# One exponential moved ahead of K's high part in ACT's queue

## The chip, the cores and the metric

The kernel runs on one core of a Trainium2 chip. The metric is device time in microseconds (us). Five engines have queues of their own and work through them strictly in order: PE (TensorE, matmuls and transposes), DVE (VectorE), ACT (ScalarE), POOL (GpSimd) and SP (which here issues DMAs). What one engine makes and another uses is guarded by semaphores.

## The reference

Attention with RMS-normed queries and keys, followed by two gated MLPs on its output:

```
q_n, k_n = rmsnorm(q, g_q), rmsnorm(k, g_k)        # 4 x 12 heads, 448 x 64
scores = 1/8 * q_n @ k_n^T
attn = exp(scores - max(scores)) ; attn /= sum(attn) + 1e-9
x = attn @ v                                       # seen as 1792 x 768
x = ((x @ w_a) * (x @ w_b)) @ w_out                # 768 -> 1536 -> 768
x = (sigmoid(x @ w_gate) * (x @ w_val)) @ w_out    # the result
```

All is float32. A float32 product is made on PE from a high and a low part of each factor (three matmuls: high by high, high by low, low by high).

## The kernel before

The attention takes two heads at a time, as a pair; there are 24 pairs. Pair i's seven score tiles of 128 queries are called t = 0 to 6: PE makes tiles t and t + 4 together in `s(i, t)` (line 373), DVE takes each tile's row maximum in `top` (line 379), and ACT takes the exponential with its row sum in `exp` (line 392). A score tile lies in one of three PSUM buffers, so the third tile after it can be begun only when its exponential is done.

K and Q of the next pair are prepared meanwhile. `t_tr(i, 1)` transposes K and `t_tr(i, 0)` transposes Q on PE into a PSUM tile `tr`; for K, ACT then takes the high part, `k_hi` (line 341, tile `KH`), and DVE the low part, `k_lo` (line 352, tile `KL`), which reads KH. For Q the same is done at lines 331 (`q_hi`) and 336 (`q_lo`).

The exponentials of the pair before are turned and multiplied with V. `x_tr(i, j)` transposes a block of them on PE (14 transposes, into another `tr`), `x_out(i, j, b)` copies the result to SBUF in two halves, tile `pt` (ACT at line 426; for two of the six halves DVE at line 424), and `pv(i, j)` multiplies it with V (line 438). All `tr` tiles come from one pool of two PSUM buffers (`ps_tr`, `bufs=2`), so each transposing step waits until what lay in its buffer has been copied out or read.

The rest of a pair is small: `total`, `rsum` and `rsum_tr` make the inverse row sums, `norm` (line 477, tile `xs`) scales a result of two pairs before, `mean` (line 253), `rsqrt` and `newton` (lines 275 to 277) make the norms of a pair two or three ahead, POOL scales Q and K (lines 286 and 299) and squares them (lines 229 to 231). `decode` puts one step of preparing the MLPs' weights (lines 724 to 731, 844, 658) on ACT or DVE, where a planner chooses.

The order of all this is written out by hand. A turn is one pass of the table `turns`, which runs for i = 2 to 22, so 21 times; in it, offset 0 is the pair whose scores are made, 1 the pair whose K and Q are prepared, -1 the pair whose exponentials are turned. Each engine gets its instructions in the table's order. The tools place the semaphore waits, and pick which of a pool's buffers a tile gets.

```
(early, 0), (early_hi, -1), (squares, 3), (total, -1), (early_lo, -1), (s, 0, 0), (t_tr, 1, 1),
(top, 0, 0), (k_hi, 1), (exp, 0, 0), (x_tr, -1, 0), (top, 0, 4), (k_lo, 1), (x_out, -1, 0, 0), (s, 0, 1),
(x_out, -1, 0, 1), (norm, -2), (rsum, -1), (decode, 0, 0), (mean, 3), (exp, 0, 4), (x_tr, -1, 1), (x_out, -1, 1, 0),
```

These are the first three rows of the table. After them come x_out(-1, 1, 1) on DVE, top(0, 1) and exp(0, 1), and so on to tile 3.

Of the kernel before, what the change touches and what calls it, by code (L numbers as in the profile page):

```python
# [23 lines left out]
def attention_then_two_gated_mlps(  # L24
# [90 lines left out]
    def attention():  # L115
# [418 lines left out]
        def warm(i, n):  # L534
# [28 lines left out]

        turns = (
            (early, 0), (early_hi, -1), (squares, 3), (total, -1), (early_lo, -1), (s, 0, 0), (t_tr, 1, 1),
            (top, 0, 0), (k_hi, 1), (exp, 0, 0), (x_tr, -1, 0), (top, 0, 4), (k_lo, 1), (x_out, -1, 0, 0), (s, 0, 1),
            (x_out, -1, 0, 1), (norm, -2), (rsum, -1), (decode, 0, 0), (mean, 3), (exp, 0, 4), (x_tr, -1, 1), (x_out, -1, 1, 0),
            (load, 4), (load_r, 3), (load_v, 1), (t_tr, 1, 0), (rsum_tr, -1), (rsum_post, -1), (put, -2),
            (pv, -1, 0), (scale, 2, 2), (x_out, -1, 1, 1), (top, 0, 1), (q_hi, 1), (scale, 2, 0), (exp, 0, 1), (pv, -1, 1),
# [836 lines left out]
    with tc.manual_schedule():  # L1406
        main = mlps()
        attention()
        open_places(6, 4, 2, 3)
        begin_mm("mm1", 3)  # L1410
        for c in range(KC):
            place(where[0]["A22"], "l", c, F32, "f")
        for n, c in (("A22", 0), ("A21", 0), ("A22", 1), ("A21", 1), ("A21", 2), ("A22", 2)):
            stage_in(0, n, c)
        for c in range(KC):
            stage_in(0, "A11", c)
        low_third(1)
        sum_third(2)
        next(main)
        cast_third(2)  # L1420
        next(main)
        next(main)
        low_third(2)
        ready[0] = True
        for _ in main:
            pass
# [29 lines left out]
```

## Time and profile before

| | |
|---|---|
| median of 3 runs | 1200.4 us (1197.67 to 1200.63) |
| the profiled execution | 1203.69 us, span 1201.9 us |
| busy, share of the span | PE 97%, DVE 77%, ACT 55%, POOL 14% |
| granted TensorE clock, mean | 0.993 |
| busy tenths of the first nine of 40 slices (30 us each) | PE 788999888, DVE 689999877, ACT 678889987 |

The attention's turns lie in the first fifth of the span. The line of K's high part (341) runs 24 times there, the last at 243.9 us. A time in a row counts from the span's start. Waits are put down to the engine that came last by the semaphores seen; where that engine had long been done, it was another.

### The profile page before, as it was taken

What the parts mean: (1) busy time and instruction counts of PE and PEld (TensorE: products, weight loads), DVE (VectorE), ACT (ScalarE), POOL (GpSimd) and SP (SyncE); (2) the same over time, 40 slices, a digit from 0 to 9 for tenths busy, and PEclk for the clock granted to TensorE, in tenths of its full rate; (3) what the DMA queues carried; (4) which work ended last, traced back from release to release, by engine and by line L of the source; (5) the groups of instructions that cost most, each with busy time, mean ns of one, the idle gap of its engine ahead of it and who ended that gap; (6) DMA issues with size and microseconds to landing.
All of it is one profiled execution on the core that took longest, in us unless ns stands there. A gap on an engine that the chain in (4) does not pass through costs nothing.

```text
span 1201.9 us, 19970 instructions
## 1 busy us (share of the span) xinstructions
PE 1162.0 (97%) x7236; PEld 1007.6 (84%) x7236; DVE 921.9 (77%) x1579; ACT 664.7 (55%) x1298; POOL 163.2 (14%) x270
## 2 busy tenths in 40 slices
PE   7889998889999999999999999999999999999998
PEld 5555555548999999999999999899999999999998
DVE  6899998777868687785768798977786877667673
ACT  6788899875634434444455656544545444445542
POOL 5666677600000000000000000000000000000000
PEclk8999999999999999999999999999999999999999
DMA  5444465348136565564955753244565654777682
GB/s 135 127 131 128 131 170 156 96 150 302 61 129 194 144 188 174 173 203 138 327 181 175 245 179 119 77 134 137 169 204 143 201 164 143 266 259 244 190 274 92
DMA packets 144370, 205.88 MB, mean 171 GB/s; under 512 B 24808, under 2 KB 118160, under 8 KB 144272
## 3 DMA queue, kind: packets, MB, share of 16 engines
q1 hardware_dynamic: 143712, 204.18, 54.3%
q8 instruction: 57, 0.93, 0.3%
q10 hardware_dynamic: 432, 0.43, 0.1%
q14 instruction: 41, 0.34, 0.1%
q0 software_dynamic: 128, 0.00, 0.0%
HBM read 150.21 MB, written 54.35 MB: 170 GB/s over the span
## 4 chain that ended last, share of the span: by engine, by line
PE 79%; ACT 5%; DVE 5%; POOL 4%; DMA 2%; issue 2%; SPq 2%; POOLq 0%; ACTq 0%; DVEq 0%
PE mm L1030 49%; PE mm L1317 13%; PE mm L1327 12%; PE pv L438 2%; ACT P L392 2%; ACT pt L426 1%; PE s L373 1%; POOL qkn L286 1%; PE tr L155 1%; POOL sq L229 1%; ACT KH L341 1%; POOL sq L231 1%; DMA rqk<-in_k_dram 1%; DVE pt L424 1%; DVE xl L658 1%
## 5 line engine op out<-in xcount | busy, mean ns | idle before, releaser
L1030 PE MATMUL mm<-xh,wh 128*128 128x448 f32 x1008 | 369.6, 367 | 0.6 <-ACT u L1082 0.4
L1030 PE MATMUL mm<-xh,wl 128*128 128x448 f32 x1008 | 369.0, 366 | 0.8 <-DVE wl L658 0.8
L1030 PE MATMUL mm<-xl,wh 128*128 128x448 f32 x1008 | 369.0, 366 | 0.0
L1030 PEld LDWEIGHTS mm<-xh,wh 128*128 128x128 f32 x1008 | 189.4, 188 | 19.7 <-issue 2.6
L1030 PEld LDWEIGHTS mm<-xh,wl 128*128 128x128 f32 x1008 | 189.5, 188 | 16.9 <-DVE wl L658 1.1
L1030 PEld LDWEIGHTS mm<-xl,wh 128*128 128x128 f32 x1008 | 189.5, 188 | 15.5
L658 DVE TENSOR_TENSOR wl<-d,wh 128x384 fp32r<-128x384 f32 x250 | 136.3, 552 | 67.1 <-ACT wh L1190 42.7
L844 ACT CAST wh<-d 128x384 fp32r<-128x384 f32 x166 | 81.9, 513 | 99.7 <-DVE d L832 75.5
L724 ACT ACTIVATE d<-raw 128x384 f32<-128x384 f32 x138 | 75.9, 555 | 76.9 <-DMA raw<-in_moe_w_out_dram 41.3
L731 DVE SCALAR_TENSOR_TENSOR d<-d,raw 128x384 uint32<-128x384 uint32 x138 | 77.6, 563 | 49.2 <-ACT d L724 43.0
L392 ACT ACTIVATE P<-s,nm 128x448 f32<-128x448 f32 x166 | 105.2, 642 | 17.0 <-DVE nm L379 16.9
L1190 ACT CAST wh<-d 128x384 fp32r<-128x384 f32 x84 | 43.2, 515 | 122.9 <-issue 40.4
L379 DVE TENSOR_REDUCE nm<-s 128x1 f32<-128x448 f32 x166 | 94.9, 616 | 11.4 <-PE s L373 10.8
L1327 PE MATMUL mm<-wh,gh 128*128 128x384 f32 x294 | 98.7, 336 | 0.2 <-ACT mm L1298 0.2
L1327 PE MATMUL mm<-wl,gh 128*128 128x384 f32 x294 | 98.6, 335 | 0.0
L1327 PE MATMUL mm<-wh,gl 128*128 128x384 f32 x294 | 98.5, 335 | 0.0
L1317 PE MATMUL mm<-gh,wl 128*128 128x448 f32 x252 | 92.0, 365 | 0.0
L1317 PE MATMUL mm<-gh,wh 128*128 128x448 f32 x252 | 92.0, 365 | 0.0
L1317 PE MATMUL mm<-gl,wh 128*128 128x448 f32 x252 | 92.0, 365 | 0.0
L727 DVE SCALAR_TENSOR_TENSOR raw<-raw 128x384 uint32<-128x384 uint32 x140 | 77.9, 556 | 4.0
L438 PE MATMUL pv<-pt,v 128*64 128x448 f32 x288 | 72.8, 589 | 4.4 <-DVE pt L424 3.3
L373 PE MATMUL s<-KH,QH 64*128 64x448 f32 (+1 forms) x166 | 56.1, 461 | 20.2 <-ACT P L392 19.9
(162 smaller groups left out, 1920.8 us busy)
## 6 DMA issues: line engine op xcount, KB each, us to landing
gd<-u SPq DMA_DIRECT2D x60, 448.0 KB
u<-gd SPq DMA_DIRECT2D x60, 448.0 KB
d<-wd SPq DMA_DIRECT2D x132, 192.0 KB
raw<-in_moe_w_out_dram SPq DMA_DIRECT2D x48, 384.0 KB
wd<-d SPq DMA_DIRECT2D x72, 192.0 KB
raw<-in_moe_w_a_dram SPq DMA_DIRECT2D x24, 384.0 KB
raw<-in_moe_w_b_dram SPq DMA_DIRECT2D x24, 384.0 KB
raw<-in_moe_w_val_dram SPq DMA_DIRECT2D x23, 384.0 KB
```

Source lines behind the costliest of these rows:

```text
L373: nc.tensor.matmul(out_, w[e, o:o + P], x[e, m:m + S], start=(n == 0), stop=(n == 2))
L379: nc.vector.tensor_reduce(out=d["nm"][:, t:t + 1], in_=d["ps"][t], axis=AX.X, op=ALU.max, negate=True)
L392: nc.scalar.activation(out=e, in_=d["ps"].pop(t), func=AF.Exp, bias=d["nm"][:, t:t + 1], accum_out=d["sum"][:, t:t + 1])
L438: nc.tensor.matmul(pvs[64 * h:64 * h + 64, o:o + S], w, x, start=(n == 0), stop=(n == R), skip_group_check=True)
L658: eng.tensor_tensor(out=lo, in0=t, in1=f32(hi), op=ALU.subtract)
L724: nc.scalar.activation(out=f32(t), in_=f32(high), func=AF.Copy, scale=2.0 ** -112)
L727: nc.vector.scalar_tensor_tensor(out=low, in0=high, scalar=0x80000000, in1=low, op0=ALU.bitwise_and, op1=ALU.bitwise_or)
L731: nc.vector.scalar_tensor_tensor(out=t, in0=t, scalar=3, in1=low, op0=ALU.logical_shift_left, op1=ALU.bitwise_or)
L844: nc.scalar.copy(out=hi, in_=t)
L1030: nc.tensor.matmul(ps[:, o:o + S], w[:, P * c:P * c + P], x[:, x0:x0 + S], start=(p in (1, 5) and c == 0 and z == 0), stop=(c == KC - 1 an ...
L1317: nc.tensor.matmul(ps[:, o:o + S], w[:, P * un:P * un + P], g[:, g0:g0 + S], start=(p in (1, 5) and f == 0 and z == 0), stop=(f == HF - 1 ...
L1327: nc.tensor.matmul(ps[:, o:o + HB], g[:, P * t:P * t + P], w, start=(p in (1, 5) and f == 0 and z == 0), stop=(f == HF - 1 and z == 2), sk ...
```

## The change

In the table `turns`, the entry for the first exponential of a pair changes places with the entry for the high part of the next pair's K. Nothing else in the text differs.

```
-            (top, 0, 0), (k_hi, 1), (exp, 0, 0), (x_tr, -1, 0), (top, 0, 4), (k_lo, 1), (x_out, -1, 0, 0), (s, 0, 1),
+            (top, 0, 0), (exp, 0, 0), (k_hi, 1), (x_tr, -1, 0), (top, 0, 4), (k_lo, 1), (x_out, -1, 0, 0), (s, 0, 1),
```

On ACT, at the start of a turn (the three exponentials at the top end the turn before; KH is K's high part, the two copies are x_out(-1, 0)):

```order
 L392 ACTIVATE P,sum<-s,nm 128x448 [waits DVE_49] x2
 L392 ACTIVATE P_282,sum<-s,nm 128x448 [waits DVE_49]
-L341 ACTIVATE KH<-tr,G 128x2x4x64 [waits PE_49,Pool_49]
-L392 ACTIVATE P,sum<-s,nm 128x448 [waits DVE_49]
+L392 ACTIVATE P,sum<-s,nm 128x448 [waits DVE_49,Pool_49]
+L341 ACTIVATE KH<-tr,G 128x2x4x64 [waits PE_49,Pool_49]
 L426 COPY pt<-tr 128x7x64 [waits PE_49]
 L426 COPY pt<-tr 128x7x64
```

The two change places, and the exponential now names POOL among what it waits for, as KH did and does.

On PE, a little later in the same turn (`s` is s(0, 1), `tr<-ident,P` is x_tr(-1, 1), `tr<-ident,qkn` is t_tr(1, 0)):

```order
 L373 MATMUL s<-KH,QL 128x448 x2
 L373 MATMUL s<-KL,QH 128x448 x2
-L155 MATMUL tr<-ident,P 128x64 [waits DVE_49,PE_49]
+L155 MATMUL tr<-ident,P 128x64 [waits PE_49,Activation_49]
 L155 MATMUL tr<-ident,P 128x64 x5
 L155 MATMUL tr<-ident,P_281 128x64 x2
 L155 MATMUL tr<-ident,P 128x64 x6
-L155 MATMUL tr<-ident,qkn 128x64 [waits PE_49,Activation_49]
+L155 MATMUL tr<-ident,qkn 128x64 [waits DVE_49]
 L155 MATMUL tr<-ident,qkn 128x64 x5
 L155 MATMUL tr<-ident,qrem 128x64 x2
```

No matmul moves, but two waits change places: x_tr(-1, 1), which waited for DVE, now waits for ACT, and t_tr(1, 0) behind it the other way round. The two `tr` buffers free at that point are the one of K's transposes, last read by KL on DVE, and the one of x_tr(-1, 0), last read by the two copies on ACT; they are handed out the other way round. DVE, POOL and SP keep their order and their waits.

## Rows read from the trace of the kernel before

**Rows 1.** Busy time by stretch: stretch, its length, PE, PEld, DVE, ACT, POOL, clock, DMA, GB/s.
```profile
26.00:262.00 236.00, 211.45 (x2366) 126.32 (x2364) 209.67 (x426) 199.20 (x555) 148.92 (x236) 0.98 0.45 133
```

**Rows 2.** PE's waits in 37 to 252 us: us in total, times, longest.
```profile
PE s L373 <- ACT P L392: 17.3, 21, 1.0
```

**Rows 3.** DVE's waits in 37 to 252 us, the same columns.
```profile
DVE nm L379 <- PE s L373: 8.5, 9, 1.3
```

**Rows 4.** Timeline of ACT, two turns: start, duration, line, out<-in, [idle before].
```profile
47.80 0.69 ACT L341 ACTIVATE KH<-tr,G 128x512 fp32r<-128x512 f32 x1 [0.94 <-POOL rc L445]
48.38 0.63 ACT L392 ACTIVATE P<-s,nm 128x448 f32<-128x448 f32 x1
...
48.99 0.97 ACT L426 COPY pt<-tr 128x448 f32<-128x448 f32 x2
...
50.49 0.53 ACT L426 COPY pt<-tr 128x448 f32<-128x448 f32 x1
...
150.85 0.63 ACT L392 ACTIVATE P<-s,nm 128x448 f32<-128x448 f32 x1
...
152.97 0.53 ACT L426 COPY pt<-tr 128x448 f32<-128x448 f32 x1
```

**Rows 5.** Timeline of DVE, the turn at 47.8 us.
```profile
47.48 1.15 DVE L379 TENSOR_REDUCE nm<-s 128x1 f32<-128x448 f32 x2 [1.04 <-PE s L373]
48.56 0.86 DVE L352 SCALAR_TENSOR_TENSOR KL<-tr,G,KH 128x256 fp32r<-128x256 f32 x2
...
50.04 0.57 DVE L253 TENSOR_REDUCE ms<-sq 128x14 f32<-128x448 f32 x1
51.05 0.62 DVE L424 COPY pt<-tr 128x448 f32<-128x448 f32 x1 [0.44 <-ACT pt L426]
```

**Rows 6.** Timeline of PE, three turns (47.8, 120.0 and 150.3 us).
```profile
49.15 0.47 PE L373 MATMUL s<-KH,QH 64*128 64x448 f32 x1 [0.76 <-ACT P L392]
...
49.67 0.66 PE L155 MATMUL tr<-ident,P 64*128 64x64 f32 x12
...
121.91 0.66 PE L155 MATMUL tr<-ident,P 64*128 64x64 f32 x12
...
152.28 0.66 PE L155 MATMUL tr<-ident,P 64*128 64x64 f32 x14
```

**Rows 7.** Instructions of lines 379 and 277: min/median/max in ns, first and last start.
```profile
L379 DVE TENSOR_REDUCE nm<-s x166: 606/614/626, 13.3 to 261.0; 128x1 f32<-128x448 f32 x166
...
L277 DVE SCALAR_TENSOR_TENSOR y<-t,y x24: 173/174/1020, 7.5 to 232.1; 128x14 f32<-128x14 f32 x24
```

**Rows 8.** Timeline, the turn at 120.0 us: DVE.
```profile
118.04 1.11 DVE L275 SCALAR_TENSOR_TENSOR t<-y 128x14 f32<-128x14 f32 x1
...
119.58 1.15 DVE L379 TENSOR_REDUCE nm<-s 128x1 f32<-128x448 f32 x2
120.76 0.87 DVE L352 SCALAR_TENSOR_TENSOR KL<-tr,G,KH 128x256 fp32r<-128x256 f32 x2
```

**Rows 9.** Timeline, the turn at 120.0 us: ACT.
```profile
120.63 0.63 ACT L392 ACTIVATE P<-s,nm 128x448 f32<-128x448 f32 x1
```

**Rows 10.** Timeline, the turn at 150.3 us: DVE.
```profile
149.27 1.02 DVE L277 SCALAR_TENSOR_TENSOR y<-t,y 128x14 f32<-128x14 f32 x1
150.20 1.14 DVE L379 TENSOR_REDUCE nm<-s 128x1 f32<-128x448 f32 x2
151.27 0.86 DVE L352 SCALAR_TENSOR_TENSOR KL<-tr,G,KH 128x256 fp32r<-128x256 f32 x2
...
153.53 0.62 DVE L424 COPY pt<-tr 128x448 f32<-128x448 f32 x1 [0.21 <-ACT pt L426]
```

**Rows 11.** Timeline of POOL, ends and starts of turns.
```profile
122.98 0.45 POOL L299 TENSOR_SCALAR qkn<-rqk,y 128x64 f32<-128x64 f32 x1 [3.23 <-PE tr L155]
...
149.07 1.18 POOL L231 TENSOR_TENSOR sq<-sq 128x448 f32<-128x448 f32 x1
```

**Rows 12.** Timeline of DVE, the turn at 211 us.
```profile
214.06 0.69 DVE L477 TENSOR_TENSOR xs<-pv,rs 128x512 f32<-128x512 f32 x1 [1.17 <-issue]
```

## The prediction

> **What bounds the kernel now.** I read the busy time by stretch first, then the waits of PE and DVE in the turns, then three turns instruction by instruction. The attention is tight on two engines: between 26 and 262 us PE is busy for 211.5 and DVE for 209.7 of 236.0 us [rows 1]. Later stages are left as they are by the change, so only the 21 turns count. In them PE's main idle time is one wait, 17.3 us in 21 times, for an exponential to free a score buffer [rows 2]. It stands before the second half of s(0, 1) [rows 6], and what frees it is the moved exp(0, 0). That wait is what the change can shorten, and I put against it what the change makes late.
>
> The turns fall into three kinds by what the first maximum, top(0, 0), waits for. In nine it waits for PE's scores, 8.5 us in all [rows 3]; the turn at 47.8 us shows one [rows 4, 5]. In the other twelve DVE goes from one turn to the next without a pause, held up shortly before by one of the three small steps of `newton`, which takes 1.02 or 1.11 us where 0.17 is usual [rows 7, 8, 10]. These are six where K's transposes are ready late and KH starts well after top(0, 0) has begun (as at 120.0 us), and six where top(0, 0) is late (as at 150.3 us).
>
> **The change, part by part.** Nothing is added or removed but one wait. On ACT, exp(0, 0) no longer stands behind KH, and KH stands behind exp(0, 0). The price of that depends on when exp(0, 0) may start, which is when top(0, 0) is done: a maximum takes 0.61 us [rows 7], and at 150.3 us exp starts 0.04 after it (150.20 + 0.61 = 150.81, start 150.85 [rows 4, 10]). ACT's spacing is read at 47.8 us: KH to what follows 0.58, exp with its sum to what follows 0.61, the two copies 0.97 together [rows 4].
>
> First kind: top(0, 0) ends at 47.48 + 0.61 = 48.09, so exp starts at 48.13 in place of 48.38, which is 0.25 sooner. KH starts at 48.13 + 0.61 = 48.74 in place of 47.80, which is 0.94 later, for ACT stood ready from before 47.80 and now idles until the maximum is there. KH ends at 49.43, so KL starts near 49.45 in place of 48.56: 0.89 later, and DVE, which is in order, stands still for it. The copies run from 49.32 to 50.29.
>
> Now PE. x_tr(-1, 1) waited for DVE and now waits for ACT, the order on PE shows: it gets the buffer which the two copies empty, not the one which KL empties. At 150.3 us it began 0.15 after KL's end (151.27 + 0.86 = 152.13, then 152.28 [rows 6, 10]). With the same 0.15 behind the copies it starts at 50.44 in place of 49.67: 0.77 later. PE has everything of the turn behind it in its queue: t_tr(1, 0), the products with V, s(0, 2), s(0, 3), and the next turn's s(0, 0). Since PE's main pause in a turn is the one before s(0, 1), there is little slack in which to win this back. On DVE the half copy x_out(-1, 1, 1) comes 0.69 + 0.56 behind the start of x_tr(-1, 1) (152.28, 152.97, 153.53 [rows 4, 6, 10]), so at 51.69 in place of 51.05, 0.64 later; a wait of 0.44 before it [rows 5] takes up the rest of KL's 0.89. With a weight step on DVE that wait is gone and 0.89 comes through. I take 0.8 for the six ordinary turns of this kind, 4.8. Three have a wait of their own behind KL, such as one of 1.17 for the row sums' transfer [rows 12], or a weight step on ACT, and lose some 0.4 together. Sum 5.2.
>
> Second kind: top(0, 0) ends at 120.19, exp starts at 120.23 in place of 120.63 [rows 8, 9], KH at 120.84, KL at 121.55 in place of 120.76 (0.79 later), and the copies end at 120.84 + 0.58 + 0.97 = 122.39, so x_tr(-1, 1) starts at 122.54 in place of 121.91 [rows 6], 0.63 later. Between 0.63 and 0.79 I take 0.7; six times, 4.2.
>
> Third kind: exp stays at 150.85, since the maximum, not KH, was last. KH goes to 151.46, KL to 152.17 in place of 151.27 (0.90 later), the copies end at 153.01, x_tr(-1, 1) starts at 153.16 in place of 152.28, 0.88 later, and x_out(-1, 1, 1), which already waited, is 0.88 later too. Three turns at 0.88 give 2.6; the three with weight casts between hide some of it, 0.7 each, 2.1. Sum 4.7.
>
> In all 5.2 + 4.2 + 4.7 = 14.1 us lost. The profiled execution took 1203.7 us, so 1217.8 on its scale; it stands 3.3 us above the median of 1200.4, and on that scale the forecast is 1214.5, rounded to 1214.
>
> The bounds. Above, all of KL's delay comes through in every turn: 9 x 0.89 + 6 x 0.79 + 6 x 0.90 = 18.1 us, 1218.5. Below, nothing of it does and the earlier exponential counts in full: 0.25 nine times and 0.40 six times, 4.65 us gained, 1195.7. The nearest rows, PE's one pause and DVE's closed ranks [rows 1, 2], put the truth near the upper end. The exponential's added wait for POOL costs nothing I can see: it can only guard the row sums' buffer, used by POOL one turn before, some 10 us back.
>
> The small steps of `newton` are the one place where lost time might be returned. In twelve turns one of them ends with POOL's last squaring step: 149.27 + 1.02 = 150.29 against 149.07 + 1.18 = 150.25 [rows 10, 11]. If DVE comes later and POOL does not, the 0.85 over the usual 0.17 [rows 7] shrinks. But POOL's work in a turn starts when t_tr(1, 0) frees its input (it idles 3.23 us for it [rows 11]), and t_tr(1, 0) stands behind x_tr(-1, 1) on PE, later by 0.63 to 0.88 as well. I count nothing.
>
> The Trainium skill, page "SBUF — State Buffer", section "Who interferes with whom", says that a DVE instruction with two SBUF inputs and a GpSimd instruction that reads SBUF hold one port pair in turn, for a whole instruction, the first to start winning. The trace agrees: these steps end with POOL's. By that rule alone, with POOL left at its times, the loss would be that of the second rival below.
>
> **The rivals.** *The earlier exponential wins.* s(0, 1) starts sooner in fifteen turns, and 4.65 us go: 1195.7. For it speaks that PE's main wait names this exponential [rows 2]. Against it: what stands behind s(0, 1) on PE is x_tr(-1, 1), and that is later by 0.63 or more; and nothing needs s(0, 1)'s scores soon, since top(0, 1) is behind KL, x_out(-1, 1, 1) and all between in DVE's queue. It decides from the point where KH costs DVE less than 0.25 us of delay. The Trainium skill, page "Perfetto Trace Analysis", section "Optimization Strategies", tells to speed up whatever an idle matmul engine waits for; applied to that wait by name it gives this rival.
>
> *POOL's hold returns it.* In the twelve turns of the second and third kind DVE's delay vanishes in newton's held step. Then 14.1 - (4.2 + 4.7) = 5.2 us stay: 1205.6. For it: 0.85 us of hold is about the delay. Against: POOL is delayed by the same chain.
>
> *All of KL's delay comes through*, 1218.5, when DVE alone sets each turn.
>
> *No change*, 1200.4: exp and KH are both off the path because waits I hold for tight, those of the nine turns [rows 3] and others like them behind, take up the delay. Against it: the wait of the nine is itself a wait for PE, which is later too.
>
> **How the numbers follow.** Forecast (near 14 us slower) 0.60, full delay 0.14, POOL's hold 0.14, no change 0.07, gain 0.05. The range that leaves out the last two and part of the others is 1205 to 1220. A measurement of this kernel can tell about 0.3%, 3.6 us, from no change. Slower: 0.60 + 0.14 + 0.14 = 0.88; within it 0.07; faster 0.05.
>
> **What would show it.** In the profile after: KH some 0.65 us behind the start of exp(0, 0) in every turn; a new wait of DVE before KL for KH, 0.8 to 0.9 us in some 20 turns; PE's wait of 17.3 us for the exponential shorter, and a new one before x_tr(-1, 1) for ACT's copies; the attention's last KH near 258 us in place of 243.9; the stage after it as long as before. The forecast is wrong if DVE's wait before KL is there but the turns keep their length (then newton's steps should show 0.17), or if KL does not wait.

## The result, and the profile after

The changed kernel takes 1217.3 us (median of 4 runs, 1216.61 to 1218.86) against 1200.5 for the kernel before, run beside it: ratio 1.0141, 95% interval 1.0126 to 1.0157, so 16.8 us slower, where the forecast was 14.1 us lost (1214) and the range 1205 to 1220. The profiled execution took 1218.86 us, its span 1217.1. Of all runs told of below one, of e9, took 1873.9 us at a mean granted clock of 0.556; the ratios leave it out.

The stage after the attention is as long as it was, 939 us here and 940 before; what is lost is lost in the turns. From the first turn's first maximum to the end of the last turn it is 232.4 us in place of 216.2. The waits in the turns, of PE first, then of DVE (engine, line, waited for: us in total, times, longest):

```profile
PE s L373 <- ACT P L392: 13.9, 21, 0.8
PE tr L155 <- ACT pt L426: 11.8, 21, 0.6
PE pv L438 <- DVE pt L424: 4.1, 12, 0.4
```

```profile
DVE KL L352 <- ACT KH L341: 18.9, 21, 0.9
DVE nm L379 <- PE s L373: 11.8, 11, 2.3
```

The wait the change is aimed at did shrink, from 17.3 to 13.9 us [rows 2]. Two new ones stand beside it, each in all 21 turns: PE waits 11.8 us for ACT's two copies before x_tr(-1, 1), and DVE 18.9 us for KH before KL. The second turn of the loop, which answers to the one at 47.8 us [rows 4, 5, 6], on ACT, DVE and PE (start, duration, engine, line, out<-in, [idle before]):

```profile
49.15 0.63 ACT L392 ACTIVATE P<-s,nm 128x448 f32<-128x448 f32 x1 [1.37 <-DVE nm L379]
49.68 0.19 ACT L392 ACTIVATION_READ_ACCUMULATOR P<-s,nm 128x1 f32 x1
49.77 0.68 ACT L341 ACTIVATE KH<-tr,G 128x512 fp32r<-128x512 f32 x1
50.34 0.96 ACT L426 COPY pt<-tr 128x448 f32<-128x448 f32 x2
```

```profile
48.43 1.16 DVE L379 TENSOR_REDUCE nm<-s 128x1 f32<-128x448 f32 x2 [1.06 <-PE s L373]
50.48 0.88 DVE L352 SCALAR_TENSOR_TENSOR KL<-tr,G,KH 128x256 fp32r<-128x256 f32 x2 [0.90 <-ACT KH L341]
51.27 0.68 DVE L477 TENSOR_TENSOR xs<-pv,rs 128x512 f32<-128x512 f32 x1
51.87 0.19 DVE L449 RECIPROCAL rc<-rc 128x7 f32<-128x7 f32 x1
51.98 0.57 DVE L253 TENSOR_REDUCE ms<-sq 128x14 f32<-128x448 f32 x1
52.61 0.62 DVE L424 COPY pt<-tr 128x448 f32<-128x448 f32 x1
```

```profile
49.92 0.47 PE L373 MATMUL s<-KH,QH 64*128 64x448 f32 x1 [0.59 <-ACT P L392]
...
51.35 0.65 PE L155 MATMUL tr<-ident,P 64*128 64x64 f32 x14 [0.56 <-ACT pt L426]
```

ACT now idles 1.37 us until the maximum is there, where before it idled 0.94 and then did KH in the rest of that time. From the start of top(0, 0): KL came 1.08 us later before and comes 2.05 now, x_tr(-1, 1) 2.19 and 2.92, the half copy on DVE 3.57 and 4.18. The turn is 10.67 us long in place of 10.06.

Those three figures were forecast at 0.89, 0.77 and 0.64 later; they are 0.97, 0.73 and 0.61. But the turns together lost more than the forecast, because of something it had not in it. Windows on PE of the changed kernel (stretch, its length, busy with count, granted clock, DMA share, GB/s):

```profile
74.00:78.00 4.00, 4.00 (x30) 0.58 0.22 66
78.00:82.00 4.00, 4.00 (x31) 1.00 0.60 155
162.00:166.00 4.00, 3.51 (x30) 0.58 0.48 119
186.00:190.00 4.00, 4.00 (x32) 0.57 0.39 122
```

Three times in the turns PE was granted 1.2 GHz for three to four us; the turn it falls in is 11.9 to 12.0 us long and not 10.6 to 10.8. The kernel before has one such stretch, between 214 and 219 us:

```profile
214.00:219.00 5.00, 4.26 (x29) 0.66 0.64 220
```

That one lies in the turn at 211 us, in which `xs` waits for the row sums' transfer [rows 12]; the turn is 12.18 us long before and 10.77 now. So the 16.2 us more in the turns are 14.0 in the other twenty, reckoned without low stretches (with e8 below for the three turns that have one), 3.7 for these stretches, and 1.4 less in the turn at 211 us.

### The profile page after: what moved, and what is told of

Read it like the earlier page. It is cut to its first block, busy times and chain, and to the rows that moved or that the text cites. A ratio compares the mean times of both kernels' runs of the same rounds, so it can differ in the third digit from the quotient of the medians.

```text
span 1217.1 us, 19969 instructions
## 1 busy us (share of the span) xinstructions
PE 1168.1 (96%) x7236; PEld 1007.0 (83%) x7236; DVE 920.2 (76%) x1579; ACT 665.9 (55%) x1298; POOL 162.8 (13%) x270
## 4 chain that ended last, share of the span: by engine, by line
PE 81%; DVE 8%; ACT 3%; DMA 3%; issue 2%; POOL 1%; SPq 1%; DVEq 0%; ACTq 0%; POOLq 0%
PE mm L1030 48%; PE mm L1317 13%; PE mm L1327 12%; PE pv L438 4%; PE s L373 2%; PE tr L155 2%; DVE nm L379 2%; ACT pt L426 1%; DVE pt L424 1%; ACT KH L341 1%; DMA qk<-in_k_dram 1%; ACT P L392 1%; DVE xl L658 1%; DVE xs L477 1%; DVE t L275 1%
## 5 line engine op out<-in xcount | busy, mean ns | idle before, releaser
L379 DVE TENSOR_REDUCE nm<-s 128x1 f32<-128x448 f32 x166 | 95.0, 617 | 14.3 <-PE s L373 13.7
L155 PEld LDWEIGHTS tr<-ident,P 64*128 64x128 f32 x1200 | 49.0, 141 | 41.4 <-ACT pt L426 19.6
```

The source lines that it names most:

```text
L155: nc.tensor.transpose(out, in_[rows[b]], ident[rows[b], rows[b]])
L379: nc.vector.tensor_reduce(out=d["nm"][:, t:t + 1], in_=d["ps"][t], axis=AX.X, op=ALU.max, negate=True)
```

## The experiments

Theory A: PE's queue sets a turn, by the start of x_tr(-1, 1). Theory B: DVE's queue does, by the start of KL. Theory C: the loss beyond the forecast is the clock. Ratios are to the kernel before on the same chip, with the 95% interval.

**e1, the buffers alone.** The order of before, but x_tr(-1, 1) is given the buffer of x_tr(-1, 0).

```
- def unit():
-     return ps_tr.tile([P, 2, 512], F32, tag="tr", name="tr")
+ def unit(same=False, n=[1]):
+     n[0] ^= not same; return ps_tr.tile(..., tag=f"tr{n[0]}", name="tr", bufs=1)
- d["X", j] = tr = unit()
+ d["X", j] = tr = unit(j == 1 and 1 <= i <= 21)
```

> The order of the kernel before, with the two transposing buffers handed out as in the changed kernel: x_tr(-1, 1) waits for ACT's two copies, t_tr(1, 0) for KL; KH and KL keep their times. Theory A (PE's queue sets a turn, so what counts is when x_tr(-1, 1) starts): it starts 0.15 us behind the copies, at 50.11 in place of 49.67, 122.35 in place of 121.91 and 152.59 in place of 152.28, so 0.44, 0.44 and 0.31 later in six turns of each kind: 7.1 us slower, near 1207.6. Theory B (DVE's queue sets a turn, so what counts is when KL starts): KL is not late, so no change, 1199 to 1202.

1202.7 us against 1200.05, ratio 1.0024 (1.0013 to 1.0035). Neither number came, though theory B's range ends just below. Fourteen of the 21 turns are longer, by some 0.2 us: 10.29 against 10.06, 10.63 against 10.42. Six are as long as before to 0.07 us, and the turn at 211 us, without a low stretch, is 1.97 us shorter. On PE, at a turn like that at 47.8 us:

```profile
49.70 0.47 PE L373 MATMUL s<-KH,QH 64*128 64x448 f32 x1 [0.76 <-ACT P L392]
...
50.56 0.65 PE L155 MATMUL tr<-ident,P 64*128 64x64 f32 x14
...
51.45 0.97 PE L438 MATMUL pv<-pt,v 128*64 128x448 f32 x4
```

The product with V in the kernel before:

```profile
50.69 2.02 PE L438 MATMUL pv<-pt,v 128*64 128x448 f32 x8
```

x_tr(-1, 1) is 0.86 behind the released half of s(0, 1), where it was 0.52 before [rows 6], so 0.34 later, yet the product with V behind it starts only 0.21 later (1.75 against 1.54). In the kernel before the first transposes run beside the last matmuls of s(0, 1); I take it that this is why some 0.1 us of the delay is free. PE's delay does lengthen a turn with KL on time, so theory B alone is out; theory A's price was too high.

**e2, the exponential alone.** The changed order with the buffers as before: the first of e1's two edits, on the changed kernel.

> The changed order of ACT, with the two buffers handed out as before: x_tr(-1, 1) waits for KL, t_tr(1, 0) for the copies. Theory A and theory B alike: KL ends at 50.32 in a turn like that at 47.8 us, x_tr(-1, 1) starts at 50.47 where the changed kernel has 50.44 by the same reckoning, so the time stays near that of the changed kernel, 1216 to 1218, with DVE's wait for KH near 19 us. The rival that the swap of the buffers is the loss: 1200 to 1204.

1223.1 us, ratio 1.0187 (1.016 to 1.0214), above what either theory gave. The swap of buffers is not the loss. x_tr(-1, 1) waits for KL instead, 0.7 us each time, and at 2.4 GHz that comes out even: some turns are 0.15 us longer than the changed kernel's (10.73 against 10.58, 10.81 against 10.66), others 0.1 to 0.15 shorter (11.06 against 11.19). What is left is the clock: seven stretches at 1.2 GHz in the turns of this profile, and each such turn is 12.05 to 12.09 us long. One of them, by window on PE, and PE's first wait:

```profile
108.00:112.00 4.00, 4.00 (x38) 0.60 0.19 58
```

```profile
PE tr L155 <- DVE KL L352: 15.0, 21, 0.7
```

**e3, KL out of DVE's way.**

```
- (top, 0, 4), (k_lo, 1), (x_out, -1, 0, 0), (s, 0, 1),
- (x_out, -1, 0, 1), (norm, -2), (rsum, -1), (decode, 0, 0), (mean, 3),
+ (top, 0, 4), (x_out, -1, 0, 0), (s, 0, 1),
+ (x_out, -1, 0, 1), (norm, -2), (rsum, -1), (k_lo, 1), (decode, 0, 0), (mean, 3),
```

> The changed kernel with KL moved on DVE behind xs and the reciprocal (0.7 us of work), so that DVE does not stand still for KH. x_tr(-1, 1) still waits for ACT's copies. Theory A: DVE's wait for KH falls from 18.9 to 2 to 5 us, but x_tr(-1, 1) stays where it is and so do the turns: 1214 to 1217. Theory B: DVE's 0.7 of 0.9 us a turn is won back in 18 to 21 turns, 12 to 15 us: 1202 to 1205.

1217.4 us, ratio 1.0141 (1.012 to 1.0161): just above theory A's range and far from theory B's. DVE's wait for KH is nearly gone, PE's is not, and what DVE saves before KL it waits out before its half copy:

```profile
PE tr L155 <- ACT pt L426: 11.9, 21, 0.6
```

```profile
DVE pt L424 <- ACT pt L426: 10.7, 18, 1.3
...
DVE KL L352 <- ACT KH L341: 3.4, 17, 0.2
```

Eight turns with a weight step on DVE did get shorter (10.91 against 11.18, 10.80 against 10.98), so there DVE was the later of the two by 0.2 to 0.3 us, 2.3 us in all. The four others with such a step that can be compared did not, and turns without one stayed, 10.67 against 10.67. The profile has four stretches at 1.2 GHz, one more than the changed kernel, and the fourth, of 7 us, is in the turn whose row sums come late: that turn takes 14.06 us against 10.77, which hides the small gain.

**e4 and e8, PE's pause filled.** Dummy transposes behind x_tr(-1, 0), in an unused corner of its buffer; e8 has the changed kernel's buffers pinned by e1's edits, while in e4 they fell to the tiles as in e2.

```
+ (fill, -1, 12),
+ def fill(i, n):
+     for x in range(n):
+         turned(st[i]["X", 0][:, x % 2, S:512], ident, x % 2)
```

> The changed kernel with 12 transposes of the identity into an unused corner of x_tr(-1, 0)'s buffer, on PE in its pause before the second half of s(0, 1); their result is not used. Theory C (2 to 3 us of the loss beyond the forecast are stretches of three to four us in which PE was granted 1.2 GHz, three in the changed kernel's profile after 70 us and one in the profile before): with the pause filled these stretches go, DVE's wait for KH stays near 19 us, and the time falls by 2 to 4 us to 1213 to 1215. Without C: no change or, if the dummies delay s(0, 1), slower, 1217 to 1222.

> The changed kernel, its two transposing buffers as there, with the 12 dummy transposes in PE's pause before s(0, 1); the earlier run with dummies had the buffers the other way round. Theory C: DVE's wait for KH stays at 18.9 us and PE's for the copies near 12, PE's wait for the exponential falls from 13.9 to about 5, and of the three stretches at 1.2 GHz at most one stays, at 1.0 to 1.3 us each: 1213.5 to 1215.5, which is the 14 us of the forecast without the rest. Without C: 1217, as the changed kernel.

e4: 1215.6 us, ratio 1.0126 (1.0106 to 1.0146), just above theory C's range, with one low stretch in the turns, that of the late row sums. e4 and e2 differ by the dummies only: 7.5 us for six stretches fewer. e8: 1215.0 us, ratio 1.0116 (1.01 to 1.0132), inside theory C's range, and no low stretch in the turns. e8's clock from 37 to 261 us, by window (its last turn ends at 265 and is at 2.4 GHz too), and its wait on DVE:

```profile
37.00:261.00 224.00, 201.47 (x2430) 1.00 0.44 127
```

```profile
DVE KL L352 <- ACT KH L341: 18.9, 21, 0.9
```

Where the changed kernel ran at 2.4 GHz, fourteen of its eighteen turns are equal to 0.05 us (10.67 and 10.67, 10.99 and 10.98) and four are 0.15 shorter; where it did not, they are 10.81 for 11.93, 10.67 for 11.89 and 10.61 for 11.97. So a low stretch costs 1.1 to 1.4 us there, and e8's loss against the kernel before is 14.2 us.

The stretches are counted in one profile of each kernel, and the intervals of e8 and of the changed kernel overlap a little; those of e4 and e2 do not. The mean granted clock of every run points the same way: 0.990 to 0.992 in the changed kernel against 0.992 to 0.997 in e8, 0.984 to 0.990 in e2 against 0.993 to 0.997 in e4.

**e6, the same dummies in the kernel before.**

```
- (x_tr, -1, 0), (top, 0, 4),
+ (x_tr, -1, 0), (fill, -1, 12), (top, 0, 4),
```

> The kernel before with the 12 dummy transposes in PE's pause before s(0, 1). Theory C: the one stretch at 1.2 GHz in the turns (214 to 219 us) goes, worth 1.0 to 1.5 us: 1198.5 to 1199.5; the turns' lengths otherwise stay at 9.8 to 10.6 us. Without C: no change, or slower if the dummies delay s(0, 1), 1200 to 1204.

1201.6 us, ratio 1.0014 (1.0003 to 1.0026): a miss. Nineteen turns are as long as before to 0.05 us, so the dummies cost nothing there, but the one low stretch came again, at 212 to 216 us, in the turn where xs waits for the row sums' transfer (1.56 us here, 1.17 before [rows 12]). What the dummies fill is not what preceded that one. It is so in all profiles: the five in which xs waits longest in that turn (1.1 to 2.1 us: before, e3, e4, e5, e6) have a low stretch in it, the six in which it waits 0 to 0.8 us have none. Why the whole is a little slower the profile does not show; the mean granted clock of e6's twelve runs is 0.994 against 0.996 in the runs of the kernel before beside them.

**e5, e7 and e9, the aim by another way.** e7: K's transposes to the end of the turn before, ahead of the last product with V. e9: that product into PE's pause. e5: both.

```
e7: - (s, 0, 0), (t_tr, 1, 1),         + (s, 0, 0),
    - (exp, 0, 6), (pv, -1, 3),        + (exp, 0, 6), (t_tr, 2, 1), (pv, -1, 3),
e9: - (x_tr, -1, 0), (top, 0, 4),      + (x_tr, -1, 0), (pv, -2, 3), (top, 0, 4),
    - (exp, 0, 6), (pv, -1, 3),        + (exp, 0, 6),
e5: e9's lines, the first of e7, and (pv, -1, 2), (t_tr, 2, 1),
```

The short tables ahead of the turns and behind them, changed to match, are left out here.

> Built on the kernel before, with KH ahead of the exponential as there: the transposes of the next K move to the end of the turn before, behind the third product with V, so that KH fills ACT's idle time before the first maximum, and the fourth product with V moves into PE's pause before s(0, 1). The exponential then starts 0.04 us behind top(0, 0), as the change wanted, and KL waits for nothing. Theory A: s(0, 0) about 0.28 us sooner and the exponential 0.25 more in the nine turns of the first kind, 0.38 in the six of the second, nothing in the six of the third: 6.8 us faster, near 1193, and up to 1.5 more if PE's one stretch at 1.2 GHz goes. Rival: DVE's queue sets the turns of the kernel before, and nothing is won: 1199 to 1201.

> The kernel before with only the transposes of the next K moved, to the end of the turn before, ahead of the fourth product with V. KH then runs before the first maximum is there. Theory A: s(0, 0) comes 0.24 us later on PE in the nine turns of the first kind, which takes back the 0.25 the exponential wins there; in the six of the second kind it wins 0.36 to 0.40: 2.3 us faster, near 1198. If neither counts: 1200; if the delay of s(0, 0) counts in all 21 turns: 5 us slower, 1205.

> The kernel before with only the fourth product with V moved into PE's pause before s(0, 1); K's transposes stay behind s(0, 0). It parts the 4.8 us that both moves together won. Theory A: s(0, 0) comes some 0.28 us sooner in the turns where PE's queue sets it, nine or ten that count, 2.5 us: 1197 to 1198. If the whole gain is this move's: 1194 to 1196. If it is K's early transposes alone that win, once they no longer push s(0, 0) back: 1199 to 1201.

e5: 1194.8 us against 1199.6, ratio 0.9958 (0.9942 to 0.9973), faster than either kernel: 4.8 us won on the kernel before, where 6.8 were expected. e9: 1198.35 against 1200.8, ratio 0.998 (0.9969 to 0.9991), half of e5's gain, as theory A had it. e7: 1206.3 against 1199.6, ratio 1.0055 (1.0036 to 1.0075), a miss, nearest to the 1205 set for a delay in all turns: the transposes ahead of s(0, 0) make DVE wait for it in all 21, not in nine:

```profile
DVE nm L379 <- PE s L373: 18.6, 21, 1.9
```

So in the twelve turns in which I took DVE for setting its own pace, s(0, 0) had less slack than the delay it got: those of the third kind are some 0.5 us longer (10.72 against 10.17), those of the second at most 0.15 (10.50 against 10.42). In e5 on ACT, at the second turn, and on PE:

```profile
45.02 0.71 ACT L341 ACTIVATE KH<-tr,G 128x512 fp32r<-128x512 f32 x1
45.97 0.63 ACT L392 ACTIVATE P<-s,nm 128x448 f32<-128x448 f32 x1 [0.23 <-DVE nm L379]
```

```profile
45.82 0.97 PE L438 MATMUL pv<-pt,rz 128*64 128x448 f32 x4
46.73 0.49 PE L373 MATMUL s<-KH,QH 64*128 64x448 f32 x2
```

KH is done before the maximum is, the exponential waits only for the maximum, and PE's pause holds a product. PE's wait for the exponential is 1.1 us in all, from 17.3; the turns of the second kind are 10.05 us in place of 10.42.

## Why the prediction was right

The mechanism was the one forecast, and so was most of its size. Step by step:

*Exponential sooner, KH later.* Right. KH starts 0.62 behind the exponential in the turn shown, and ACT idles before the exponential: the waits of that line for DVE are 39.1 us in 42 times, from 12.9 in 21. The last KH is at 260.9 us, where 258 was forecast.

*KL's delay.* DVE waits 18.9 us for KH in 21 turns, where the upper bound had 18.1. This wait is not the loss by itself: e3 takes away most of it and the time stays. It counts in eight turns with a weight step on DVE, by 0.2 to 0.3 us a turn, 2.3 us in all.

*x_tr(-1, 1) behind the copies.* Right in time (0.73 later at a turn like that at 47.8 us, 0.77 forecast). The 0.15 us I set behind the copies is 0.05 (copies end 51.30, PE starts 51.35); 0.15 is what PE takes behind DVE: in e2, where x_tr(-1, 1) waits for KL, 0.145 in all 21 turns. And some 0.1 us of delay is free (e1). Of the six ordinary turns of the first kind four lost 0.6, not 0.8, and two with a weight step on DVE 0.93 and 0.94; of the three set at some 0.4 together two lost 0.1 and 0.4, and the third is the turn at 211 us. The six of the second kind lost 0.55 to 0.83 (0.7 forecast), those of the third 0.63 to 0.86 (0.7 to 0.88 forecast), where e8 stands in for the three turns with a low stretch.

*The sum.* 14.1 us were forecast; with no low stretch in the turns e8 lost 14.2. Turn by turn e8's profile lost 13.7 us in the twenty turns other than that at 211 us: 4.8 in those of the first kind, 4.1 in the second, 4.8 in the third, where 5.2 (for nine), 4.2 and 4.7 were forecast. That the sums agree to 0.1 us is in part luck: the ordinary turns of the first kind came out 0.5 us below their term, and the kernel before has a low stretch of its own in its profile.

*What was left out.* The clock, 2.3 us between the medians of e8 and the changed kernel, three stretches at 1.2 GHz in the latter's profile. The sum had no term for it: I took durations at 2.4 GHz throughout and did not ask what more pauses do to the clock. PE's waits in the turns, added up, are 20.8 us before and 30.0 after. With the turn at 211 us set apart, low stretches stand only in the three profiles in which PE waits longest in all:

| | before | e1 | after | e2 | e3 | e4 | e8 | e6 | e7 | e9 | e5 |
|---|---|---|---|---|---|---|---|---|---|---|---|
| PE's waits in the turns, us | 20.8 | 18.7 | 30.0 | 29.5 | 27.8 | 23.7 | 22.1 | 12.9 | 21.0 | 6.0 | 6.6 |
| stretches at 1.2 GHz there, but for the turn at 211 us | 0 | 0 | 3 | 7 | 3 | 0 | 0 | 0 | 0 | 0 | 0 |
| in the turn at 211 us | 1 | 0 | 0 | 0 | 1 | 1 | 0 | 1 | 0 | 0 | 1 |

*The rivals.* The earlier exponential won nothing here; in e5, where KH does not pay for it, it does. POOL's hold returned little: of newton's steps 11 take 1.0 us or more in the changed kernel and 14 in e8, against 13 before, with POOL's squaring step later too. One turn on DVE and on POOL:

```profile
125.10 1.11 DVE L275 SCALAR_TENSOR_TENSOR t<-y 128x14 f32<-128x14 f32 x1
```

```profile
125.04 1.14 POOL L231 TENSOR_TENSOR sq<-sq 128x448 f32<-128x448 f32 x1
```

That agrees again with what the Trainium skill, page "SBUF — State Buffer", section "Who interferes with whom", says of the port pair, and with the argument that both engines hang on the same transposes. That all of KL's delay comes through was too high, since PE's path is shorter.

What stays open: why low stretches come where they do. No pause of PE in the changed kernel's turns lasts over 0.84 us, where the kernel before has pauses of up to 1.04, and most turns with both pauses kept 2.4 GHz.

## What to carry to other kernels

A wait named for an instruction does not say that moving this instruction up its queue is free: ask what it passes, whether the passed work was filling idle time, and who is behind that work on the other engines. Here KH ran in time that ACT had to wait anyway, and putting it behind the wait made work on three engines 0.6 to 1.0 us later in the turn, and the turn itself mostly 0.6 to 0.9 us longer. Filling the wait with work that is ready, and starting the passed work earlier still, brought what the swap was after.

## What the runs showed that I had not expected

Two short pauses of PE, 0.66 and 0.56 us a turn, came with stretches at 1.2 GHz that cost 1.1 to 1.4 us each, and in the profiles with dummy transposes in one of the two pauses these were gone: three to none between the changed kernel and e8, seven to one between e2 and e4, and that one has the late row sums before it. Which of two free PSUM buffers a tile gets changed with the order of two instructions on another engine, and in the kernel before that is worth 0.2 us in two turns of three.
